# First half of w_in loaded in four pieces, V of the sixth pair behind a gate, three filler matmuls ahead of the first FFN product

## The chip, the cores and the metric

One core of one Trainium2 chip runs the whole program. The metric is the device time of one launch in microseconds (us). Before the change it is 332.88 us, the median of three runs (332.18 to 333.69).

## What is computed

A windowed attention with eight global tokens feeds a feed-forward layer (FFN) with a squared ReLU. Inputs and output are float32; the kernel works in bf16 on TensorE.

```python
# q, k, v: (8, 8, 576, 64); global_idx: 8 of the 576 positions
scores = q @ k.T / 8
mask = |i - j| <= 32  or  i is global  or  j is global
attn = softmax(where(mask, scores, -1e9)) @ v
x = attn.transpose(0, 2, 1, 3).reshape(4608, 512)
h = x @ w_in                              # w_in: (512, 2048)
out = (s * relu(h) ** 2 + b) @ w_out      # w_out: (2048, 512)
```

## The kernel before, in words

The 64 heads are 32 pairs (`NPAIR`), eight batches of four pairs. For each pair K and Q are brought into transposed form, `qk` (L666) makes the scores, ACT takes their exponential and DVE multiplies them by the mask (L673, L674), and `pvq` (L690) multiplies by V, two pairs at a time, in two column blocks, first with a block of ones (`onesb`) for the row sums, then with `vring`, the V of five pairs in bf16. The result is scaled into `xt` (L737), x transposed, 128 rows of the model dimension by tokens, in four row blocks `a`. The eight global tokens are put into `xt` by `scatter` on POOL (L762), eight copies per call.

The FFN runs beside the attention: `moe_quanta` (L770 to L860) is a generator of small portions. For each of nine blocks of 512 tokens there are sixteen products `psh` with `w_in` (L785, four matmuls each, over the row blocks `a`), a ReLU on ACT, a square on DVE, and then the products `pso` with `w_out` (L826). In the first block the products f = 0 to 3 are begun early: four portions ("leads") take the row blocks a = 0, 1, as soon as the first two pairs are in `xt`, and the row blocks 2, 3 follow later.

The order of each engine's work is that of the code (manual schedule). The opening (L1037 to L1165) is written out by hand: pairs 0 to 3, then `put_out(1, 1)`, two leads, `select(4)`, `trans_a(5)`, a lead, `qk(4, 0)`, a lead, `trans_b(5)`, `select(5)`, `qk(4, 1)`, a lead. From pair 4 on a table of steps rules (`run_pair`; eight steps per pair, one FFN portion in most). In that table `VLOAD`, `VROUND` and `VGLOBAL` say in which (pair, step) V of a pair is loaded on SP's queue, rounded to bf16 on POOL, and given its global rows.

DMA: POOL's queue (software, q0) brings the weights and the early K and Q with a cast to bf16; SP's queue (hardware, q1) brings V and the later K and Q. Both hold at most eight transfers in flight: each issue waits for the landing of the one eight before it. `win_t[0]` holds the columns 0 to 1023 of w_in (f = 0 to 7), `win_t[1]` the others; each is loaded in two pieces, row blocks 0, 1 (g = 0) and row blocks 2, 3 (g = 1). A `gate` is a DMA of one element on SP's queue that reads what an engine writes, so that what stands behind it in the queue starts only after that. V of pairs 4 and 5 is staged in two slots of `natk`; ACT rounds V of pair 5 at step (5, 2) (`cast_v`, L332). `warm(n)` (L989 to L993) issues n matmuls of zeros of 512 columns into an idle bank.

The names that matter below: `psv`, `psx`, `po` (L554, L690) are the last attention products ahead of the leads; `gf`, `gb`, `psg` (L415, L531, L539) are the gathered global rows of K and Q of the second group of pairs, their rounding on DVE and their transposes on TensorE, at step (7, 7); `gvall` is the V of the global rows.

Of the kernel before, what the change touches and what calls it, by code (L numbers as in the profile page):

```python
# [48 lines left out]
    8: (7, 0), 9: (7, 3), 10: (9, 0), 11: (9, 3), 12: (10, 4), 13: (11, 0), 14: (12, 3), 15: (12, 7),  # L49
# [3 lines left out]
    (12, 1): (1, 13), (13, 4): (1, 14), (14, 0): (1, 15),  # L53
}
VGLOBAL = {
    8: (8, 6), 9: (9, 0), 10: (10, 5), 11: (10, 7), 12: (12, 0), 13: (12, 3), 14: (13, 7), 15: (14, 2),
# [48 lines left out]
def kernel(  # L105
# [100 lines left out]
    win_t = [wpool.tile([P, 4, DF // 2], BF16, name=f"win{i}", tag=f"win{i}") for i in range(2)]  # L206
    wout_t = wpool.tile([P, 16, DM], BF16)
# [148 lines left out]
    gate = const.tile([1, 2], BF16)  # L356
# [8 lines left out]
    for p in range(6):  # L365
        load_v(nc.sync, p)
        if p == 3:
            nc.sync.dma_start(
                out=natk[0:NG, 2:4].rearrange("p n c h d -> p (n c h d)"),
                in_=bass.AP(  # L370
                    tensor=v.tensor, offset=v.offset,
                    ap=[[2 * NCH * 2 * D, NG], [1, 2 * NCH * 2 * D]],
                ),
            )
# [395 lines left out]
    def moe_quanta():  # L770
        for t in range(NTOK // 512):
# [10 lines left out]
            def into(psh, f, heads):  # L782
                for a in heads:
                    for j, (x0, d0, n) in enumerate(cols):
                        nc.tensor.matmul(  # L785
                            psh[:, d0 : d0 + n],
                            win_t[f // 8][:, a, 2 * P * (f % 8 // 2) :][:, 0 : 2 * P]
                            .rearrange("p (x t) -> p t x", t=2)[:, f % 2],
                            xt[:, a, x0 : x0 + n],
                            start=(a == 0 and j == 0), stop=(a == 3),  # L790
                            skip_group_check=True,
                        )
# [235 lines left out]
    def load_w_in(j, parts):  # L1028
        x = slice(1024 * j, 1024 * j + 1024)
        for g in parts:  # L1030
            nc.gpsimd.dma_start(out=win_t[j][:, 2 * g : 2 * g + 2], in_=w_in2[:, g, :, x])

# [12 lines left out]
    load_w_in(0, (0,))  # L1045
    load_kq(5)
    load_w_in(0, (1,))
# [51 lines left out]
    load_w_in(1, (0,))  # L1099
    muls[2]()  # L1100
    mask_b()
    gv_out()
    scatter(0, 0)
    warm(2)
# [15 lines left out]
    load_w_in(1, (1,))  # L1120
# [4 lines left out]
    open_batch(1)  # L1125
    lead()
# [19 lines left out]
    nc.sync.dma_start(out=gate[:, 1:2], in_=xgs[0][0:1, 2, 0:1])  # L1146
# [175 lines left out]
```

## Time and profile before

| | before |
|---|---|
| median of three runs | 332.88 us (332.18 to 333.69) |
| the profiled execution, its own time | 333.04 us |
| its span, first to last instruction | 331.1 us |
| TensorE (PE) busy | 317.5 us, 96% of the span |
| VectorE (DVE) busy | 210.0 us, 63% |
| ScalarE (ACT) busy | 197.3 us, 60% |
| GpSimd (POOL) busy | 121.4 us, 37% |
| moved by DMA | 49.48 MB, mean 149 GB/s |
| mean granted TensorE clock | 0.983 of full speed |

The profile is of one execution, 0.16 us above the median; its span leaves 1.94 us of its time outside. A busy share is an average over stages with different limits: TensorE is busy nearly throughout, but a matmul at half the clock is busy for twice as long, so the granted clock has to be read beside the busy time. "Idle before" names how long an engine stood still before an instruction and what ended that.

### The profile page before, as it was taken

How to read it: one execution, taken by the hardware profiler on the slowest of the kernel's cores; microseconds unless marked ns; L12 is line 12 of the kernel's file. 1: busy time of each engine (PE TensorE's matmuls, PEld its weight loads, DVE VectorE, ACT ScalarE, POOL GpSimd, SP SyncE). 2: the span in 40 equal slices, each digit the busy share in tenths (PEclk: the TensorE clock that was granted, in tenths of full speed). 3: DMA queues.
4: the chain of work that ended last, by engine and by line, in shares of the span. 5: the costliest groups of instructions: out<-in, count | busy, mean ns of one | idle time of the engine just before them, and what ended most of it. 6: DMA issues, size and time to landing. Idle time of an engine off the chain costs nothing.

```text
span 331.1 us, 8894 instructions
## 1 busy us (share of the span) xinstructions
PE 317.5 (96%) x3429; PEld 169.9 (51%) x3466; DVE 210.0 (63%) x539; ACT 197.3 (60%) x332; POOL 121.4 (37%) x237
## 2 busy tenths in 40 slices
PE   7977999999999999999999999999999999999996
PEld 5753445445454544478544444444466544444444
DVE  6893777687865885587568666776676624323422
ACT  3873885559865786678656875786378306404700
POOL 7397424221513542356344235845560220000000
PEclk9995799999999999999999999999999999999999
DMA  8999999999999999999999959997970210011012
GB/s 150 182 191 208 209 201 195 198 184 173 191 175 191 215 192 191 221 177 177 182 211 159 130 103 238 226 192 148 131 181 2 95 66 32 2 64 63 2 45 82
DMA packets 125674, 49.48 MB, mean 149 GB/s; under 512 B 114168, under 2 KB 119736, under 8 KB 125624
## 3 DMA queue, kind: packets, MB, share of 16 engines
q1 hardware_dynamic: 94030, 27.49, 50.8%
q0 software_dynamic: 31248, 21.00, 35.6%
q8 instruction: 27, 0.44, 0.6%
q10 hardware_dynamic: 354, 0.43, 0.5%
q14 instruction: 15, 0.12, 0.1%
HBM read 42.22 MB, written 9.44 MB: 156 GB/s over the span
## 4 chain that ended last, share of the span: by engine, by line
PE 84%; DMA 8%; SPq 2%; issue 2%; DVE 1%; ACT 1%; POOL 1%; POOLq 0%
PE psh L785 38%; PE pso L826 34%; PE po L690 5%; PE pss L666 3%; DMA win<-in_moe_w_in_dram 3%; DMA vring<-gvall 2%; DMA natv<-in_v_dram 2%; DMA sixk<-in_k_dram 1%; SPq L246 1%; PE psw L666 1%; PE pst L616 1%; PE pst L610 1%; ACT em L673 0%; PE pst L973 0%; POOL vring L332 0%
## 5 line engine op out<-in xcount | busy, mean ns | idle before, releaser
L785 PE MATMUL psh<-xt,win 128*128 128x512 bf16 (+4 forms) x687 | 132.3, 344 | 3.3 <-DMA win<-in_moe_w_in_dram 1.8
L826 PE MATMUL pso<-wout_t,g 128*128 128x512 bf16 (+1 forms) x573 | 126.5, 373 | 2.4 <-issue 2.1
L808 ACT ACTIVATE r<-psh 128x512 bf16<-128x512 f32 x144 | 85.9, 600 | 57.2 <-PE psh L785 45.0
L785 PEld LDWEIGHTS <-win 128*128 128x128 bf16 x704 | 63.8, 99 | 60.3 <-issue 3.3
L826 PEld LDWEIGHTS <-g 128*128 128x128 bf16 x592 | 56.1, 98 | 62.8
L811 DVE TENSOR_TENSOR g<-r 128x512 bf16<-128x512 bf16 x144 | 60.9, 428 | 33.6 <-ACT r L808 32.9
L674 DVE TENSOR_TENSOR em<-em,mask 128x904 bf16<-128x904 bf16 (+1 forms) x64 | 40.2, 632 | 35.8 <-ACT em L673 30.8
L673 ACT ACTIVATE em<-pss 128x840 bf16<-128x840 f32 (+1 forms) x37 | 32.7, 883 | 44.6 <-PE pss L666 44.6
L848 DVE SCALAR_TENSOR_TENSOR osb<-pso,sb,wst 128x512 f32<-128x512 f32 (+1 forms) x21 | 15.2, 724 | 28.0 <-PE pso L826 27.8
L246 POOL DMA_DIRECT2D vring<-in_v_dram x33 | 29.5, 897 | 8.6 <-PE po L690 7.0
L737 DVE TENSOR_TENSOR xt<-po,rep 128x480 bf16<-128x480 f32 (+2 forms) x60 | 24.5, 449 | 3.3 <-ACT rep L747 3.3
L762 POOL COPY xt<-xg 128x4 bf16 (+1 forms) x72 | 17.4, 242 | 15.9 <-DVE xt L737 12.0
L673 ACT ACTIVATE em<-psw 128x904 bf16<-128x904 f32 x23 | 21.2, 924 | 0.0
L1165 POOL DMA_DIRECT2D wst<-in_moe_w_out_dram x16 | 9.1, 575 | 31.7 <-DVE wsum L1171 23.5
L666 PEld LDWEIGHTS <-kt 64*128 64x128 bf16 x384 | 12.2, 100 | 15.4 <-issue 12.3
L332 POOL CAST vring<-natv 128x640 bf16<-128x640 f32 x12 | 8.7, 723 | 31.0 <-DMA natv<-in_v_dram 19.8
L690 PE MATMUL po<-em,vring 128*32 128x160 bf16 (+3 forms) x840 | 18.1, 221 | 0.9 <-POOL vring L566 0.5
L1183 POOL DMA_DIRECT2D out_dram<-osbh x13 | 7.4, 570 | 31.6 <-DVE osbh L1182 30.9
L257 ACT CAST natb<-natk 128x640 bf16<-128x640 f32 x22 | 15.9, 724 | 0.9 <-DMA natk<-in_k_dram 0.9
L744 ACT ACTIVATE ln<-po 128x324 f32<-128x324 f32 (+1 forms) x30 | 12.9, 430 | 4.5 <-PE po L690 4.5
L666 PE MATMUL pss<-qt,kt 64*128 64x192 bf16 (+4 forms) x222 | 14.4, 243 | 1.0 <-DVE grow L402 0.4
L747 ACT ACTIVATE rep<-ln 128x324 f32<-128x324 f32 (+1 forms) x32 | 14.8, 462 | 0.4
(128 smaller groups left out, 267.6 us busy)
## 6 DMA issues: line engine op xcount, KB each, us to landing
natk<-in_k_dram SPq DMA_DIRECT2D x45, 150.0 KB, 21.8
natv<-in_v_dram SPq DMA_DIRECT2D x28, 150.0 KB, 4.9
natq<-in_q_dram SPq DMA_DIRECT2D x55, 75.0 KB, 4.8
wst<-in_moe_w_out_dram POOLq DMA_DIRECT2D x16, 256.0 KB, 4.2
out_dram<-osbh POOLq DMA_DIRECT2D x13, 256.0 KB, 3.3
out_dram<-osb POOLq DMA_DIRECT2D x12, 256.0 KB, 3.0
natq<-in_q_dram SPq DMA_DIRECT2D x9, 288.0 KB, 6.5
vring<-in_v_dram POOLq DMA_DIRECT2D x31, 75.0 KB, 4.6
```

Of the source, the lines that this page charges most:

```text
L246: eng.dma_start(out=dst[r : r + rows, n, c : c + nch, hh], in_=bass.AP(tensor=src[t].tensor, offset=o + c * KC * D, ap=[[D, rows], [KC * D ...
L257: (nc.gpsimd.tensor_copy if p == NSIX else nc.scalar.copy)(out=natb[:, p % NV].rearrange("p (c h d) -> p c h d", c=NCH, h=2), in_=natk[:, ...
L666: nc.tensor.matmul(ps[:, hh, at : at + hi - lo], ktile[p][r, P * c : P * c + P], qbufs[p % 3][r, lo:hi], start=at == 0, stop=at + hi - lo ...
L673: nc.scalar.activation(em[:], ps[:, :, 0:n], AF.Exp, scale=SCALE)
L674: later.append(lambda: nc.vector.tensor_mul(em[:], em[:], masks[g]))
L690: nc.tensor.matmul(po[DH * j : DH * j + DH, a : a + n], view(vring[:, p % NVR, c, hh, part - 1 :], [2, DH]) if part else onesb[:], emt[(p, ...
L737: nc.vector.tensor_tensor(out=view(xt[:, 2 * g, x0 + t0 :], [NXT, 2], [w, runs], [1, w]), in0=view(po[:, STEP[blk] + col :], [STEP[blk], 2 ...
L762: nc.gpsimd.tensor_copy(out=xt[:, h, S * (bi % NX) : S * (bi % NX) + S][:, :, ds(greg_p[i], 1)], in_=xgs[bi][:, h, i : i + 1],)
L785: nc.tensor.matmul(psh[:, d0 : d0 + n], win_t[f // 8][:, a, 2 * P * (f % 8 // 2) :][:, 0 : 2 * P] .rearrange("p (x t) -> p t x", t=2)[:, f ...
L808: nc.scalar.activation(r[:], psh, AF.Relu)
L811: later.append(lambda g=g, r=r: nc.vector.tensor_mul(g[:], r[:], r[:]))
L826: nc.tensor.matmul(pso[:, 0:nn], gl[f][:, u * P : u * P + P], wout_t[:, f, n0 : n0 + nn], start=(f == 0), stop=(f == 15),)
```

## The change

The first half of w_in comes in four pieces instead of two: by row blocks (g) and by 512 columns (c). In `win_h` each piece is one contiguous stretch of `win_t[0]`; f = 0 to 3 read c = 0, f = 4 to 7 read c = 1. The first two pieces stand where the two old ones stood on POOL, the third where the first piece of the second half stood, the fourth and that first piece behind `scatter(0, 0)`. V of pair 5 is taken out of the opening's loads and put behind a gate on the first half of the global results of batch 0 (`xgs[0]`). Three fillers stand on TensorE between `put_out(1, 1)` and the first lead. For pair 13 V is loaded, rounded and given its global rows one to two steps earlier.

```diff
 VLOAD = {
-    8: (7, 0), 9: (7, 3), 10: (9, 0), 11: (9, 3), 12: (10, 4), 13: (11, 0), 14: (12, 3), 15: (12, 7),
+    8: (7, 0), 9: (7, 3), 10: (9, 0), 11: (9, 3), 12: (10, 4), 13: (10, 7), 14: (12, 3), 15: (12, 7),
 }
 VROUND = {
...
-    (12, 1): (1, 13), (13, 4): (1, 14), (14, 0): (1, 15),
+    (12, 0): (1, 13), (13, 4): (1, 14), (14, 0): (1, 15),
 }
 VGLOBAL = {
-    8: (8, 6), 9: (9, 0), 10: (10, 5), 11: (10, 7), 12: (12, 0), 13: (12, 3), 14: (13, 7), 15: (14, 2),
+    8: (8, 6), 9: (9, 0), 10: (10, 5), 11: (10, 7), 12: (12, 0), 13: (12, 2), 14: (13, 7), 15: (14, 2),
 }
...
+    win_h = win_t[0][:].rearrange("p a f -> p (a f)").rearrange("p (c a f) -> p c a f", c=2, a=4)
...
-    for p in range(6):
+    for p in range(5):
         load_v(nc.sync, p)
...
-                            win_t[f // 8][:, a, 2 * P * (f % 8 // 2) :][:, 0 : 2 * P]
+                            (
+                                win_t[1][:, a, 2 * P * (f % 8 // 2) :]
+                                if f > 7
+                                else win_h[:, f // 4, a, 2 * P * (f % 4 // 2) :]
+                            )[:, 0 : 2 * P]
...
-    def load_w_in(j, parts):
-        x = slice(1024 * j, 1024 * j + 1024)
-        for g in parts:
+    def load_w_in(j, g, c=None):
+        if c is None:
+            x = slice(1024 * j, 1024 * j + 1024)
             nc.gpsimd.dma_start(out=win_t[j][:, 2 * g : 2 * g + 2], in_=w_in2[:, g, :, x])
+            return
+        x = slice(DM * c, DM * c + DM)
+        nc.gpsimd.dma_start(out=win_h[:, c, 2 * g : 2 * g + 2], in_=w_in2[:, g, :, x])
...
     cast_v(G, 2)
-    load_w_in(0, (0,))
+    load_w_in(0, 0, 0)
     load_kq(5)
-    load_w_in(0, (1,))
+    load_w_in(0, 1, 0)
...
     put_v(G, 3)
-    load_w_in(1, (0,))
+    load_w_in(0, 0, 1)
     muls[2]()
     mask_b()
     gv_out()
+    nc.sync.dma_start(out=gate[:, 1:2], in_=xgs[0][0:1, 0, 0:1])
+    load_v(nc.sync, 5)
     scatter(0, 0)
+    load_w_in(0, 1, 1)
+    load_w_in(1, 0)
     warm(2)
     put_out(1, 0)
...
     load_kq(6, "q")
-    load_w_in(1, (1,))
+    load_w_in(1, 1)
...
     open_batch(1)
+    fill[0] = bank("psf")
+    warm(3)
     lead()
     lead()
```

**TensorE, between the last products of pair 3 (`psx`) and the first lead (`psh`).** The words in brackets name what a row waits for: a DMA of POOL's queue (DMASW), POOL, ACT. Before:

```order
L690 LDWEIGHTS vring
L690 MATMUL psx<-em_625,vring 32x136
L785 LDWEIGHTS win_122 [waits DMASW1_49]
L785 MATMUL psh<-xt,win_122 128x512 [waits Pool_49]
L785 LDWEIGHTS win_122
```

Now:

```order
L691 MATMUL psx<-em_623,vring 32x136
L998 LDWEIGHTS dummy
L998 MATMUL psf<-dummy 128x512
L998 LDWEIGHTS dummy
L998 MATMUL psf<-dummy 128x512
L998 LDWEIGHTS dummy
L998 MATMUL psf<-dummy 128x512
L786 LDWEIGHTS win_122 [waits Activation_49,DMASW1_49]
L786 MATMUL psh<-xt,win_122 128x512 [waits Pool_49]
```

Three fillers that wait for nothing stand ahead of the lead, which still waits for one piece of w_in and for POOL's eight copies into `xt`.

**POOL, at the end of the first `scatter` (`xt<-xg`; ISA rows set its column).** Before:

```order
L762 COPY xt<-xg_736 128x2 [waits Pool_49]
L219 DMA sixk<-in_k_dram 96x2x384 [waits DMASW6_49,PE_49]
L762 ISA
L762 COPY xt<-xg_736 128x2 [waits DVE_49]
L762 ISA
```

Now:

```order
L763 COPY xt<-xg_734 128x2 [waits Pool_49]
L1039 DMA win_122<-in_moe_w_in_dram 128x2x512 [waits DMASW6_49]
L1036 DMA win_123<-in_moe_w_in_dram 128x2x1024 [waits DMASW7_49]
L220 DMA sixk<-in_k_dram 96x2x384 [waits DMASW0_49,PE_49]
L763 ISA
L763 COPY xt<-xg_734 128x2 [waits DVE_49]
```

Two issues of w_in stand between the first and the second `scatter` that were ahead of the first before (one of them as a whole piece).

**SP's queue, at the end of the opening's loads of V (`natk` holds V of pairs 4 and 5).** Before:

```order
L246 DMA natk<-in_v_dram 120x5x64 [waits DMAHW2_49]
L246 DMA natk<-in_v_dram 120x5x64 [waits DMAHW3_49]
L375 DMA natk<-in_v_dram 8x1280 [waits DMAHW4_49]
L1146 DMA gate<-xg 1x1 [waits DMAHW5_49,DVE_49]
L246 DMA natv<-in_v_dram 120x5x64 [waits DMAHW6_49,Pool_49]
```

Now:

```order
L376 DMA natk<-in_v_dram 8x1280 [waits DMAHW2_49]
L1111 DMA gate<-xg 1x1 [waits DMAHW3_49,DVE_49]
L247 DMA natk<-in_v_dram 120x5x64 [waits DMAHW4_49]
L247 DMA natk<-in_v_dram 120x5x64 [waits DMAHW5_49]
L1160 DMA gate<-xg 1x1 [waits DMAHW6_49,DVE_49]
L247 DMA natv<-in_v_dram 120x5x64 [waits DMAHW7_49,Pool_49]
```

The two transfers of V of pair 5 have moved behind a gate of their own, and the old gate follows them.

## Rows read from the trace of the kernel before

**Rows 1.** The page's granted TensorE clock, tenths of full speed, 40 slices of 8.3 us.
```profile
PEclk9995799999999999999999999999999999999999
```

**Rows 2.** Stretches: us, busy per engine (x instructions), PEclk, DMA share, GB/s.
```profile
14.00:18.00 4.00, 3.60 (x82) 2.88 (x86) 3.00 (x7) 2.93 (x5) 3.14 (x5) 1.00 1.01 217
20.00:22.00 2.00, 1.15 (x34) 0.63 (x24) 1.92 (x8) 1.82 (x5) 1.94 (x4) 1.00 0.99 180
24.00:26.00 2.00, 0.73 (x38) 0.52 (x37) 1.44 (x7) 1.93 (x5) 1.34 (x7) 1.00 1.17 196
26.00:28.00 2.00, 1.04 (x3) 0.43 (x4) 1.07 (x4) 0.00 (x0) 1.29 (x5) 0.58 1.20 212
28.00:36.00 8.00, 7.78 (x94) 3.83 (x94) 3.09 (x11) 3.44 (x5) 6.26 (x13) 0.50 1.18 214
```

**Rows 3.** TensorE's timeline, 24 to 38 us: start, us, instruction [idle before, releaser].
```profile
24.35 0.57 PE L690 MATMUL psx<-em,vring 128*32 128x92 bf16 x28
26.74 0.61 PE L785 MATMUL psh<-xt,win 128*128 128x512 bf16 x1 [1.83 <-DMA win<-in_moe_w_in_dram]
...
37.05 0.37 PE L666 MATMUL pss<-qt,kt 64*128 64x160 bf16 x6
```

**Rows 4.** The chain that ended last, at full clock: start, us, what.
```profile
37.42 1.83 PE psh L785 x8
39.25 0.29 PE pss L666 x6
39.54 0.38 PE pst L616 x12
...
41.99 0.38 PE pst L973 x24
```

**Rows 5.** POOL's timeline, 18 to 30 us.
```profile
18.20 0.73 POOL L1031 DMA_DIRECT2D win<-in_moe_w_in_dram  x1
...
22.35 0.72 POOL L1031 DMA_DIRECT2D win<-in_moe_w_in_dram  x1
23.20 2.51 POOL L762 COPY xt<-xg 128x2 bf16 x8
...
27.16 1.97 POOL L762 COPY xt<-xg 128x2 bf16 x8 [0.47 <-DVE xt L737]
```

**Rows 6.** DMA issues at 18.2 and at 22.35 us: KB, us to landing.
```profile
win<-in_moe_w_in_dram POOLq DMA_DIRECT2D x1, 512.0 KB, 8.5
...
win<-in_moe_w_in_dram POOLq DMA_DIRECT2D x1, 512.0 KB, 11.5
```

**Rows 7.** Around the second group's global rows: POOL, DMA issues of 50 to 55 us, DVE, TensorE.
```profile
50.83 0.56 POOL L1227 DMA_DIRECT2D gvall<-in_v_dram  x1 [1.94 <-DMA wout_t<-in_moe_w_out_dram]
...
55.87 1.64 POOL L1227 DMA_DIRECT2D gvall<-in_v_dram  x3 [2.44 <-DMA wout_t<-in_moe_w_out_dram]
...
gvall<-in_v_dram POOLq DMA_DIRECT2D x3, 6.0 KB, 5.9
...
59.74 0.22 DVE L531 CAST gb<-gf 128x128 bf16<-128x128 f32 x1
...
60.02 0.25 PE L539 MATMUL psg<-ident,gb 64*64 64x64 bf16 x4
```

**Rows 8.** V, K, gate: DVE's and ACT's timeline, two DMA issue groups, one TensorE wait.
```profile
22.02 0.40 DVE L730 TENSOR_TENSOR xg<-tot,rec 128x16 bf16<-128x16 f32 x1
...
38.49 0.74 ACT L332 CAST vring<-natk 128x640 bf16<-128x640 f32 x1
...
60.23 0.72 ACT L257 CAST natb<-natk 128x640 bf16<-128x640 f32 x1 [0.86 <-DMA natk<-in_k_dram]
...
68.95 0.87 ACT L673 ACTIVATE em<-pss 128x840 bf16<-128x840 f32 x1 [4.22 <-PE pss L666]
...
natk<-in_v_dram SPq DMA_DIRECT2D x4, 150.0 KB, 5.9
...
natk<-in_k_dram SPq DMA_DIRECT2D x45, 150.0 KB, 21.8
...
PE po L690 <- DMA vring<-gvall: 0.4, 1, 0.4
```

More of the change, by code (lines that the diff above doesn't have):

```diff
@@ L355 @@
     load_kq(1)
-    gate = const.tile([1, 2], BF16)
+    gate = const.tile([1, 3], BF16)
     nc.sync.dma_start(out=gate[:, 0:1], in_=six["k"][0:1, 1, 0, 0, 0:1])
@@ L1145 @@
     lead()
-    nc.sync.dma_start(out=gate[:, 1:2], in_=xgs[0][0:1, 2, 0:1])
+    nc.sync.dma_start(out=gate[:, 2:3], in_=xgs[0][0:1, 2, 0:1])
     load_v(nc.sync, 6)
```

## The prediction

> **What bounds the kernel now.** I read the slices of the page first. TensorE is busy from end to end except in the first 33 us, and there the row of the granted clock falls: 0.5 in the fourth slice and 0.7 in the fifth, that is somewhere between 25 and 41 us, and full speed in every slice after [rows 1]. So the program is bound by TensorE, and the one place where TensorE works badly is the opening. The stretches sharpen it: 1.00 up to 26 us, 0.58 between 26 and 28, 0.50 from 28 to 36 [rows 2]. That is the step from 2.4 to 1.2 GHz. Ahead of the fall TensorE did little: 1.15 us of 2 between 20 and 22, and 0.73 us of 2 between 24 and 26, the emptiest stretch; from 28 on it was busy 7.78 of 8 us, all at half speed [rows 2].
>
> The timeline tells why it was empty. The last `psx` products end at 24.92; the first lead starts at 26.74, after 1.83 us of waiting for the first piece of w_in [rows 3]. That piece was issued at 18.20 and took 8.5 us [rows 5, 6]: 26.7. So one late DMA costs 1.8 us itself, and the half clock behind it costs more. From the first lead to the first score product of pair 5, whose start is 37.05, TensorE needs 10.3 us [rows 3].
>
> **The same work at full clock.** Sixteen `psh` matmuls, two `select`, two sets of transposes, two `qk`. Eight `psh` take 1.83 us, a `qk` 0.29, a set of transposes 0.38, a `select` 0.38 [rows 4]. Sum: 2 x 1.83 + 2 x 0.29 + 2 x 0.38 + 2 x 0.38 = 5.8 us, against 10.3.
>
> **The change, step by step.**
>
> *First piece of half the size.* 256 KB instead of 512 behind the same queue. It cannot land earlier than half of 8.5 us after 18.20, at 22.5, nor later than the whole one, at 26.7. I take 24.5, the middle, because V of pair 5 no longer competes then. The lead has a second condition: the eight copies of `scatter(0, 0)`, which run from 23.20 to 25.71 [rows 5]. The issue of the third piece in front of them replaces one of the same 0.72 us, so they stay. The lead starts at 25.75: **1.0 us** earlier. Only a landing after 25.7 would take from this.
>
> *Three fillers.* No operand to wait for, so they start at 24.92. Eight matmuls of this width take 1.83 us [rows 4], three take 0.7: 24.92 to 25.6, in a hole that exists anyway. They cost nothing, and what covers them is the wait for the copies; if copies and piece came earlier, the price is at most 0.7 us. What they buy: the stretch from 24 to 26 then has 0.73 + 0.7 + 0.25 = 1.7 us of work in 2, more than the 1.15 us of 20 to 22, at which the clock stayed at 1.00 [rows 2]. I take it that the clock holds. This is the main term.
>
> *The trace against a rule on transposes.* Between 14 and 18 us, with transposes and narrow products and hardly anything wide, the clock stayed at 1.00 [rows 2]; the work behind the leads is of the same mix with wide matmuls added, so I expect it to hold there too. The row of 28 to 36 us, nearly full and still at 0.50, leaves a doubt. The Trainium skill ("TensorE: Matmul & The Clock Gate", Part 4: PE-mode transpose) states that transposes do not count as TensorE activity in the way matmuls do; by that rule the clock could fall behind the fillers as well, among the transposes of pair 5, and the sum would keep 1.0 us only. That is in the third case below.
>
> *Two more issues on POOL, and two moved.* The fourth piece and the first piece of the second half now stand behind the first `scatter`: 2 x 0.72 us ahead of K of pair 6 and of the second `scatter`. It started at 27.16 after 0.47 us of idling, and took 1.97 [rows 5]; POOL was free for it at 26.7. Now it is free at 26.7 + 1.45 = 28.15, and done at 30.1 to 30.2. TensorE wants it for the lead on row blocks 2, 3: 25.75 + half the psh (1.83) + the other 2.1 = 29.7. So a new wait of **0.5 us**, ending on POOL. The eight matmuls left (1.83) end at 32.0, against 37.1 before: **5.0 us** earlier.
>
> *The later pieces.* Queue order in bytes is as before up to the first piece of the second half, which landed at 22.35 + 11.5 = 33.85 [rows 5, 6]. The fourth quarter lies 512 KB ahead of that. From 26.7 to 33.85 the queue moved K and Q of pair 5 (144 KB each) and two pieces of w_in, 1.3 MB in 7.15 us, so 512 KB take 2.8 us: the fourth quarter lands at 31.0, against 32.3 when f = 4 wants it. Even at 33.85 the wait would be 1.5 us, and what follows takes more than that back anyway. I charge nothing.
>
> *V of pair 5.* Its two transfers of 150 KB leave the stretch before 23 us and return behind the gate, when the first global results of batch 0 are written, at 22.4 [rows 8]. No bytes are saved; they move out of the way of the first piece. Transfers of V took 5.9 us to land, the longest of SP's K loads 21.8 [rows 8]; nearest is V itself. Landing is then about 30, and ACT rounds it at 38.49 before [rows 8], at 33.5 now: hidden. The old gate waits for a result that comes no earlier than before, so the loads behind it keep their place.
>
> *Pair 13.* TensorE waited 0.4 us for its global rows [rows 8]. They are issued a step earlier and ahead of 300 KB of V of pair 14, so I take the whole **0.4 us** back (bounds 0 and 0.4).
>
> **What is late next.** Five microseconds ahead, TensorE meets the DMA queues, which work near their limit: 212 to 214 GB/s here [rows 2], and the change saves no byte. POOL's queue goes on delivering in the same order at the same rate. The place where this binds first is the gathered K and Q of the second group of pairs (`gf`). They stand on the queue between the last piece of w_out, whose landing released POOL at 55.87, and the `gvall` row issued at 50.83, which landed after 5.9 us, at 56.7 [rows 7]. So `gf` lands between 55.6 and 56.7; I take 56.3. Before, nobody felt it: DVE rounded at 59.74, the transposes `psg` ran at 60.02 [rows 7]. Now TensorE would come to `psg` at 55.0; with the landing at 56.3 and 0.3 us from rounding to transposes it gets there at 56.6. Of the 5.0 us, **3.4** remain (3.0 to 4.1 over the bounds), whatever small waits occur before.
>
> Behind it ACT waits longer for K of pair 10: it came 0.86 us late for a cast at 60.23 [rows 8] and will be 4.3 us late. ACT has an idle stretch of 4.2 us ahead of 68.95 [rows 8], so most of that is covered. For this and for loads up to 125 us I charge **0.5 us** (0 to 2).
>
> **Sum.** 3.4 + 0.4 - 0.5 = 3.3 us less than the profiled execution's 333.04: **329.7 us**. (Its 333.04 is 0.16 above the median.)
>
> **The rivals.**
>
> *Loads keep up.* If the queues deliver earlier because TensorE asks earlier, `gf` does not bind and 5.0 + 0.4 us stay: 327.6. For: SP's queue waits for engines at many places, above all later. Against: POOL's queue does not wait for TensorE in the opening, so its landings have no reason to move. Chance 0.12.
>
> *The clock falls all the same*, at the same place or among the transposes of pair 5. Then some 10 us at half speed stay and only the earlier start counts: 333.04 - 1.0 = 332.0. For: 28 to 36 us [rows 2], and three narrowly sized fillers. Against: the 20 to 22 us row. Chance 0.18.
>
> *The supply takes it back*: the clock holds, but K, Q and V of pairs 8 to 15 are as late as before, and ACT's 4.3 us are covered by half only. 333.04 - 3.8 + 2.2 = 331.4. For: the cast at 60.23 already waits. Against: it is the only such wait of ACT on a load in the table period that I find, and TensorE's own sum of waits for DMA there is 0.4 us. Chance 0.07.
>
> *V of pair 5 comes late: slower.* Its issue moves behind 22.4, and with the gate and two issues of some 0.7 us each the second transfer is out at 23.9; from then it shares with POOL's queue. If it needs what the slow K loads needed, 21.8 us [rows 8], it lands at 45.7; ACT, which works in order, stands at the cast from 38.5 on, the exponentials and ReLUs behind it, and TensorE with them: 7 us lost against before, about 340. It decides from a landing of 38.5 on, that is 14.6 us from issue. For: the slow loads went through the same queue. Against: V in the same opening took 5.9 [rows 8], and behind it in the queue nothing older is left. Chance 0.05.
>
> **How the numbers follow.** Likeliest, with chance 0.58: 329.7, its own range 328.5 to 331.5, from the bounds of `gf` (3.0 to 4.1), all or nothing of the 0.4, and up to 1.5 of the 2 us for later loads. The range for 8 in 10 takes in the fallen clock (332.0 with 0.2 for its spread) and reaches to 327.7, half into the case in which all is kept: 327.7 to 332.2. A measurement of this kernel tells about 0.5% from no change, 1.7 us: 331.2 and 334.5 are the marks. Faster: 0.58 + 0.12 and a little of the third rival, 0.72. Slower: 0.05 and a remainder, 0.06. The same: 0.22, nearly all of it the fallen clock.
>
> **What would show it.** Right: granted clock 1.00 in every slice after 24 us; fillers at 24.9; first lead at 25.7 to 25.8, released by POOL's copies and not by w_in; pair 5's first score product near 32; a wait of TensorE or DVE that ends on `gf` at 56 to 57; no wait for `vring` of pair 13. Wrong on the main term: a stretch at 0.50 after 26 us. Wrong on the clamp: `psg` well before 56. Wrong on V: an ACT cast of `natk` near 34 that waits for a DMA.

## The result, and the profile after

The changed kernel takes 333.90 us (median of 22 runs, 332.46 to 335.72), the kernel before, run beside it, 331.65 (22 runs, 329.19 to 334.52). The ratio is 1.0062, with a 95% interval of 1.0041 to 1.0083: **slower by 0.6%**, where 329.7 us were forecast and 332.2 was the end of the range. The profiled execution of the changed kernel took 334.58 us, its span is 332.9. The medians here and below are of all runs, while the ratios leave out four single runs that lie over 1.5% above the fastest of their kernel (two of six in e16, one of twelve in e13 and in e20).

The opening went as foretold. The page's row of the granted clock has no dip any more (before: [rows 1]):

```profile
PEclk9999999999999999999999999999999999999999
```

The stretches of the changed kernel (us, busy time of each engine, PEclk, DMA share, GB/s), against [rows 2]:

```profile
22.00:24.00 2.00, 1.78 (x66) 1.24 (x67) 1.97 (x6) 0.92 (x3) 1.81 (x4) 1.00 1.06 123
24.00:26.00 2.00, 1.46 (x43) 0.93 (x42) 1.48 (x6) 1.97 (x5) 1.52 (x8) 1.00 1.23 187
26.00:28.00 2.00, 2.00 (x42) 1.10 (x40) 1.66 (x10) 0.23 (x2) 2.00 (x3) 1.00 1.21 215
28.00:36.00 8.00, 6.30 (x78) 3.08 (x78) 5.34 (x13) 7.17 (x13) 6.39 (x16) 1.00 1.18 202
```

From 24 to 36 us every stretch has 1.00, the higher of the two levels, where the profiled execution of the kernel before had 0.50. But the last column is new: from 22 to 24 us the DMA engines are as busy as ever (share 1.06) and move 123 GB/s. In the kernel before, the same two microseconds had 1.08 and 198 GB/s:

```profile
22.00:24.00 2.00, 1.44 (x52) 1.06 (x53) 1.98 (x5) 0.85 (x3) 1.82 (x4) 1.00 1.08 198
```

TensorE's timeline of the changed kernel (start, us, instruction, idle before and releaser), against [rows 3] and the `psg` row of [rows 7]:

```profile
25.19 0.59 PE L998 MATMUL psf<-dummy 128*128 128x512 bf16 x2 [0.16 <-issue]
25.88 1.02 PE L786 MATMUL psh<-xt,win 128*128 128x512 bf16 x4
...
30.39 1.67 PE L786 MATMUL psh<-xt,win 128*128 128x512 bf16 x7 [0.17 <-POOL xt L763]
32.20 0.37 PE L667 MATMUL pss<-qt,kt 64*128 64x160 bf16 x6
...
36.33 0.45 PE L617 MATMUL pst<-ident,sixk 96*64 96x96 bf16 x12 [1.40 <-DMA sixk<-in_k_dram]
...
58.00 0.25 PE L540 MATMUL psg<-ident,gb 64*64 64x64 bf16 x4 [0.88 <-DVE gb L532]
```

The first lead starts at 25.88 and not at 26.74, pair 5's first score product at 32.20 and not at 37.05: 4.85 us ahead. At `psg` 2.0 of them are left (58.00 against 60.02), although DVE's cast ahead of it now waits for `gf` itself:

```profile
57.67 0.27 DVE L532 CAST gb<-gf 128x128 bf16<-128x128 f32 x1 [0.70 <-DMA gf<-in_q_dram,grow]
```

Behind it the lead turns into a lag. The first `psw` product of pairs 11, 12 and 14 in the kernel before, by TensorE's timeline:

```profile
91.07 0.37 PE L666 MATMUL psw<-qt,kt 64*128 64x160 bf16 x6
...
97.84 0.36 PE L666 MATMUL psw<-qt,kt 64*128 64x160 bf16 x6
...
114.81 0.36 PE L666 MATMUL psw<-qt,kt 64*128 64x160 bf16 x6
```

and in the changed kernel:

```profile
91.97 0.37 PE L667 MATMUL psw<-qt,kt 64*128 64x160 bf16 x6
...
100.22 0.36 PE L667 MATMUL psw<-qt,kt 64*128 64x160 bf16 x6
...
116.58 0.37 PE L667 MATMUL psw<-qt,kt 64*128 64x160 bf16 x6
```

0.90 us behind at pair 11, 2.38 at pair 12, 1.77 at pair 14, and 1.78 at the last such product (249.63 against 247.85). So 6.6 us are lost between 32 and 115 us, and nothing after it. TensorE's four longest waits from 28 to 110 us name where 5.1 of them go (us in total, times, longest):

```profile
PE psw L667 <- DVE kt L578: 1.6, 2, 0.9
PE pst L617 <- DMA sixk<-in_k_dram: 1.4, 1, 1.4
PE po L691 <- DMA vring<-gvall: 1.2, 1, 1.2
PE psg L540 <- DVE gb L532: 0.9, 1, 0.9
```

In the kernel before, the only wait for a load there is the 0.4 us of [rows 8].

### The profile page after: what moved, and what is told of

The parts are those of the page before. It is cut to its first block, busy times and chain, and to the rows that moved or that the text cites. A ratio compares the mean times of both kernels' runs of the same rounds, so it can differ in the third digit from the quotient of the medians.

```text
span 332.9 us, 8905 instructions
## 1 busy us (share of the span) xinstructions
PE 315.7 (95%) x3431; PEld 169.4 (51%) x3469; DVE 209.7 (63%) x539; ACT 197.8 (59%) x332; POOL 124.1 (37%) x239
## 4 chain that ended last, share of the span: by engine, by line
PE 74%; DMA 10%; SPq 6%; issue 3%; POOL 3%; DVE 1%; ACT 1%; POOLq 0%; DVEq 0%; ACTq 0%
PE pso L831 33%; PE psh L786 32%; PE po L691 5%; DMA sixk<-in_k_dram 4%; SPq L247 4%; DMA natk<-in_k_dram 3%; DMA natv<-in_v_dram 2%; PE pss L667 2%; DMA vring<-gvall 2%; SPq L287 1%; PE psw L667 1%; POOL win L1039 1%; ACT r L813 1%; POOL xt L763 1%; PE pst L611 1%
## 5 line engine op out<-in xcount | busy, mean ns | idle before, releaser
L786 PE MATMUL psh<-xt,win 128*128 128x512 bf16 (+4 forms) x687 | 129.3, 340 | 1.3 <-issue 0.3
L675 DVE TENSOR_TENSOR em<-em,mask 128x904 bf16<-128x904 bf16 (+1 forms) x64 | 39.4, 621 | 35.4 <-ACT em L674 33.0
L691 PEld LDWEIGHTS <-vring 128*32 128x32 bf16 x896 | 14.1, 99 | 2.3 <-issue 1.4
```

The costliest lines, as they stand in the source:

```text
L675: later.append(lambda: nc.vector.tensor_mul(em[:], em[:], masks[g]))
L691: nc.tensor.matmul(po[DH * j : DH * j + DH, a : a + n], view(vring[:, p % NVR, c, hh, part - 1 :], [2, DH]) if part else onesb[:], emt[(p, ...
L786: nc.tensor.matmul(psh[:, d0 : d0 + n], (win_t[1][:, a, 2 * P * (f % 8 // 2) :] if f > 7 else win_h[:, f // 4, a, 2 * P * (f % 4 // 2) :]) ...
```

## The experiments

Times are medians, and each ratio is to runs of the kernel before on the same chip. A landmark that all profiles have is the first `psw` product of a pair.

### Which part of the change costs

**e1**, the changed kernel with V of pair 5 back in the opening:

```diff
-    for p in range(5):
+    for p in range(6):
...
-    nc.sync.dma_start(out=gate[:, 1:2], in_=xgs[0][0:1, 0, 0:1])
-    load_v(nc.sync, 5)
```

> The changed kernel with V of pair 5 back among the opening's loads and without its gate; all else as changed. Theory S (supply: the DMA engines bind from about 30 to 107 us, and the gate left them short of work between 20 and 24 us, 162 and 123 GB/s against 180 and 198 before, some 0.24 MB or 1.2 us): 1.0 to 1.6 us faster than the changed kernel, and the transposes of K of pair 9, issued at 62.4 in the changed kernel, are issued near 61. Theory T (the table edits for pair 13 are what costs): within 0.4 us of the changed kernel.

Measured: 334.61 us, ratio 1.0092 (1.0055 to 1.0129). Nothing is regained. The hole in the rate, that is the stretch with few GB/s, is still there at another place: 116 GB/s from 28 to 30 us in place of 123 from 22 to 24. V of pair 5 behind its gate is not the loss.

**e2**, the changed kernel with the three entries of pair 13 as before:

```diff
-    ... 12: (10, 4), 13: (10, 7), ...
+    ... 12: (10, 4), 13: (11, 0), ...
...
-    (12, 0): (1, 13), ...
+    (12, 1): (1, 13), ...
...
-    ... 13: (12, 2), ...
+    ... 13: (12, 3), ...
```

> The changed kernel with the three table entries for pair 13 as they were before. Theory T (V of pair 13 now stands on SP's queue ahead of the global rows of pair 11, for which TensorE waited 1.25 us at 92.7): that wait goes, and the time falls by 0.8 to 1.3 us. Theory S: TensorE is held by the DMA supply as a whole, the wait comes back at a later load of the same stretch, and less than 0.5 us is won.

Measured: 333.06, ratio 1.0041 (1.0016 to 1.0065), 0.8 below the changed kernel. TensorE's wait for `gvall` rows is 0.2 us instead of 1.2. The two ratios alone do not tell the kernels apart, since their intervals overlap. The runs of e1 to e4, all on one chip, do: the fifteen with the entries (e1, e4) have a mean 1.1 us above the twenty-four without (e2, e3), with a 95% interval of 0.4 to 1.7, though the four differ in V of pair 5 and in the fillers as well. The entries cost; they were credited with a gain.

**e3**, the four pieces and the fillers alone (the edits of e1 and e2 together):

> Only the four pieces of w_in and the three fillers, V of pair 5 and the table as before. Theories S and T together: 2.0 to 2.8 us faster than the changed kernel, so at or a little under the kernel before. If the held clock were worth its full 4.5 us after all and nothing else bound: 4 us under the kernel before.

Measured: 333.29, ratio 1.0042 (1.0017 to 1.0068). So most of the loss against the kernel before is in the pieces.

**e4**, the changed kernel without `fill[0] = bank("psf")` and `warm(3)`:

> The changed kernel without its three fillers. Theory C (the held clock is worth what the stretch at half clock cost, some 4.5 us): the clock falls again after 26 us and the time rises by 3 to 5 us. Theory S: even if the clock falls, TensorE only arrives later at waits for DMA that it has anyway, and the time stays within 0.7 us of the changed kernel.

Measured: 334.29, ratio 1.0066 (1.0038 to 1.0093), level with the changed kernel. Its first lead starts no earlier or later than in the changed kernel, and without fillers the row shows what it waited for:

```profile
25.89 1.02 PE L786 MATMUL psh<-xt,win 128*128 128x512 bf16 x4 [0.84 <-POOL xt L763]
```

In five of its eight runs the mean granted clock was 0.998 or more, in two 0.990 or less; these two took 333.34 and 334.84 us, no more than the others. So in these two runs a fallen clock cost nothing that shows. Two of eight is also not far from the third of the runs in which the clock of the kernel before falls (46 of 136, below): eight runs do not tell whether the earlier lead helps the clock.

### The edits on the kernel before

**e5**, the kernel before with six fillers ahead of the first lead and nothing else:

```diff
     open_batch(1)
+    fill[0] = bank("psf")
+    warm(6)
     lead()
```

> The kernel before with nothing but six fillers ahead of the first lead (six, since its wait there is longer). It holds the clock in every run. Theory C (the held clock is worth its 4.5 us): 3 us or more under the median before. Theory S (the DMA engines bind to about 107 us, and the runs of before that keep their clock by themselves are only about 1.2 us faster than those in which it falls): 0.2 to 0.6 us under the median before, and TensorE waits at K of pair 9 and V of pairs 8 and 9 as it does in the changed kernel.

Measured: 331.16, ratio 0.9977 (0.9956 to 0.9999): a version that beats the kernel before by little (the interval ends just short of 1) and the changed one clearly. Its lead starts at 26.62, no earlier than before, and its first score product of pair 5 comes at 32.57. Its waits from 28 to 110 us:

```profile
PE psg L539 <- DVE gb L531: 1.5, 1, 1.5
PE pss L666 <- ACT em L673: 0.4, 1, 0.4
PE po L690 <- DVE xt L737: 0.2, 1, 0.2
```

2.1 us, against 5.1 in the four rows of the changed kernel. The held clock alone gives this much, and the rest of the change takes it away.

**e6**, the kernel before with the first piece of the second half moved behind the scatter:

```diff
-    load_w_in(1, (0,))
     muls[2]()
...
     scatter(0, 0)
+    load_w_in(1, (0,))
```

> The kernel before with one line moved: the first piece of the second half of w_in is issued behind the first scatter instead of ahead of it; pieces whole, no fillers, V of pair 5 and the table as before. Theory D (dry queue: with 0.5 to 0.77 MB of w_in issued only behind the scatter, POOL's DMA queue runs out of work between 23 and 30 us, and the DMA engines never get that time back): DMA moves 0.1 to 0.3 MB less between 20 and 36 us than before, and the time rises by 0.7 to 1.5 us. Theory P (the smaller pieces with rows half as long cost DMA time): no change, within 0.4 us.

Measured: 331.87, ratio 0.9995 (0.9969 to 1.0021), and 3.35 MB moved from 20 to 36 us: the expected loss did not come. One whole piece may stand behind the scatter.

**e7**, e3 with the fourth piece and the first of the second half issued ahead of the scatter:

```diff
     load_w_in(0, 0, 1)
+    load_w_in(0, 1, 1)
+    load_w_in(1, 0)
...
     scatter(0, 0)
-    load_w_in(0, 1, 1)
-    load_w_in(1, 0)
```

> The kernel of e3_win_fill (four pieces, fillers) with the fourth piece and the first piece of the second half issued ahead of the first scatter instead of behind it. The scatter and with it the first lead start some 1.4 us later, near 27.3. Theory D: the queue no longer runs dry, 3.2 to 3.3 MB between 20 and 36 us, and the time falls by 0.8 to 1.6 us against e3_win_fill in spite of the later lead. Theory P: as slow as e3_win_fill, or slower by the later lead.

Measured: 332.29, ratio 1.0014 (0.9989 to 1.0039), 1.0 below e3, and 3.13 MB from 20 to 36 us. The intervals overlap, so that the place of the two issues is about half of the loss is likely, and not shown by this run alone. A hole is left: 128 GB/s at a share of 1.06 from 22 to 24 us.

**e8**, four pieces, but each two where the whole one stood, V and pair 13 as before:

```diff
     load_w_in(0, 0, 0)
+    load_w_in(0, 0, 1)
     load_kq(5)
     load_w_in(0, 1, 0)
+    load_w_in(0, 1, 1)
...
-    load_w_in(0, 0, 1)
+    load_w_in(1, 0)
...
     scatter(0, 0)
-    load_w_in(0, 1, 1)
-    load_w_in(1, 0)
```

> As e7_issues_ahead, but each pair of quarter pieces stands where the whole piece stood before (both column halves of row blocks 0, 1, then of row blocks 2, 3), the second half in its old place. Theory D: as the kernel before, within 0.5 us. Theory P: 1.0 us or more slower than the kernel before, as e3_win_fill is.

Measured: 331.32, ratio 1.0003 (0.9975 to 1.0030); its runs spread from 329.90 to 334.27, so the ratio says more than the median. I read it as "small pieces cost nothing", and that was too quick: its profile has 3.18 MB from 20 to 36 us against 3.36 in e5, and its interval leaves room for 0.9 us.

### Bytes, runs and order

A run is a stretch of consecutive addresses within a transfer. The sizes of runs, pieces and packets are those of the bf16 numbers that land; in DRAM, where w_in is float32, the same run is twice as long.

Up to here I thought that POOL's queue ran dry while POOL did the scatter. The rows speak against it. All packets of the changed kernel from 22 to 24 us, and those of POOL's queue (packets, MB, share of the 16 engines):

```profile
DMA packets 286, 0.25 MB, mean 123 GB/s; under 512 B 20, under 2 KB 285, under 8 KB 285
...
q0 software_dynamic: 285, 0.23, 103.2%
```

and of the kernel before from 28 to 30 us, where POOL's queue is alone as well:

```profile
DMA packets 222, 0.42 MB, mean 212 GB/s; under 512 B 15, under 2 KB 15, under 8 KB 222
...
q0 software_dynamic: 222, 0.42, 112.9%
```

By their share the engines are full both times. 285 packets at 103% of 16 engines in 2 us are 116 ns each, for 0.8 KB; 222 at 113% are 163 ns each, for 1.9 KB: in the first stretch a byte costs 1.7 times as much. Short runs by themselves do not do that. The next two microseconds of the changed kernel, 24 to 26 us, have nothing but short packets of POOL's queue either:

```profile
DMA packets 446, 0.37 MB, mean 187 GB/s; under 512 B 31, under 2 KB 446, under 8 KB 446
...
q0 software_dynamic: 446, 0.37, 122.6%
```

These are 88 ns each for 0.8 KB, 1.2 times the price of a byte in the long runs. So a hole takes short runs and something else beside them; the runs below show that the time of the issues matters, and no run shows by what mechanism.

**e13**, the changed kernel with the pieces read in runs of 2 KB:

```diff
-        x = slice(DM * c, DM * c + DM)
-        nc.gpsimd.dma_start(out=win_h[:, c, 2 * g : 2 * g + 2], in_=w_in2[:, g, :, x])
+        nc.gpsimd.dma_start(
+            out=win_h[:, c, 2 * g : 2 * g + 2].rearrange("p a f -> p (a f)"),
+            in_=w_in2[:, g, c, 0 : 2 * DM],
+        )
```

> The changed kernel with its four pieces in their places and of their sizes, but each read from DRAM as runs of 2 KB (1024 columns of one row) in place of two runs of 1 KB (512 columns of two rows). The weights that land are then not the ones of the reference: it is a kernel for the time alone. Theory R (the short runs cost: in the changed kernel's 22 to 24 us 285 packets, nearly all under 2 KB, held the 16 engines for 103% of the time and carried 0.25 MB, in the kernel before 222 packets of about 2 KB carried 0.42 MB at 113% from 28 to 30 us; that is 116 ns for a short packet and 163 ns for a long one, so 1024 short ones in place of 512 long ones take 7.4 us of the 16 engines in place of 5.2): the hole at 22 to 24 us fills, 20 to 36 us carry some 3.2 to 3.3 MB in place of 2.99, and the time falls by 1.0 to 2.2 us, to 331.7 to 332.9. Theory D (POOL's queue has too little ahead of the first scatter, the issue times decide): nothing changes, 333.9 and 2.99 MB.

Measured: 333.26, ratio 1.0047 (1.0021 to 1.0073), 3.11 MB: half of what theory R (short runs cost) expected in bytes, and 0.6 us where it expected 1.0 or more. By its interval the time need not have changed.

**e14**, e5 with whole pieces of the first half, read in runs of 1 KB:

```diff
+            if not j:
+                nc.gpsimd.dma_start(
+                    out=win_t[0][:, 2 * g : 2 * g + 2].rearrange("p a (c f) -> p (a c) f", c=2),
+                    in_=w_in2[:, g].rearrange("p h (c f) -> p (h c) f", c=2)[:, :, 0:DM],
+                )
+                continue
```

> The kernel before with the six fillers ahead of the first lead (331.2 us), its first half of w_in still in two pieces of 512 KB where they stood, but each read as runs of 1 KB (512 columns of each 1024) in place of 2 KB. The second 512 columns are not the reference's: it is a kernel for the time alone. Theory R: the bytes of 20 to 36 us fall from 3.36 to about 3.0 MB, and the time rises by 1.0 to 2.2 us, to 332.2 to 333.4. Theory D: the same issues at the same times, so 331.2 and 3.36 MB.

Measured: 330.74, ratio 0.9970 (0.9949 to 0.9992), 3.32 MB. Short runs by themselves cost nothing that can be told where the other pieces stand early and whole. R alone falls.

**e9**, e5 with 0.52 MB more on POOL's queue in pair 6:

```diff
+        if p == 6:
+            wpieces(0)
```

> The kernel before with the six fillers (331.2 us) and two loads more of 256 KB each on POOL's queue at the start of pair 6, into buffers that are loaded again later and which nothing reads in between; the output is the reference's. If the DMA engines set the pace from 35 to 107 us, 0.52 MB at 204 GB/s take 2.6 us of it, of which TensorE's own work may still hide some: 331.7 to 333.8. If the transfers have room there and only single waits count, 331.2 within 0.4.

Measured: 333.50, ratio 1.0054 (1.0029 to 1.0078): 2.3 us more than e5 by the medians (2.3 and 2.8 more than e11 and e14, which ran on the same chip as e9), where the bytes at 204 GB/s, the rate of the kernel before from 28 to 60 us, are 2.6. Its longest waits from 28 to 110 us are for a transposed K and for w_in:

```profile
PE psw L666 <- DVE kt L577: 1.8, 1, 1.8
PE psh L785 <- DMA win<-in_moe_w_in_dram: 0.8, 1, 0.8
```

The clock fell for a while in that profile (0.83 from 66 to 76 us), but the six runs with a mean clock of 0.998 or more have a median of 333.01, so the price is not the clock's. That gives the frame: with TensorE at full clock, transfers set the pace here, and bytes put on POOL's queue at pair 6 cost nearly their whole time.

**e11**, e5 with the gather of `gf` ahead of the last piece of w_out:

```diff
     load_kq(8)
+    gather(1)
     load_w_out(3)
...
-                if i == 2:
-                    gather(1)
```

> The kernel before with the six fillers (331.2 us), and the global rows of the next batch (the gather into gf) issued ahead of the last load of w_out in place of behind two global rows of V. In the kernel with the fillers TensorE's one long wait from 28 to 110 us is 1.5 us at psg for those rows. If that wait is a loss of its own: psg without it, and 329.7 to 330.5. If the DMA engines are what binds, the 1.5 us come back at later loads: 331.2 within 0.4.

Measured: 331.17, ratio 0.9980 (0.9955 to 1.0006), e5's time. The wait at `psg` is gone, and waits for `kt` (0.8 us), w_in (0.7) and `gvall` (0.5) stand in its place: which load comes late can be chosen, not that one does.

**e15**, e7 with e13's runs of 2 KB, that is both halves of the loss mended in one kernel:

> The kernel of four pieces and fillers with the fourth piece and the first of the second half issued ahead of the first scatter, as it ran at 332.29 us and 3.13 MB from 20 to 36 us, its four pieces now read in runs of 2 KB (the weights that land are not the reference's: for the time alone). If late issues (0.17 MB) and short runs (0.12 MB) are two losses that add up: 3.25 to 3.35 MB, and 331.2 to 331.8, level with the kernel before with fillers (331.2). If one of them hides the other: 3.13 MB and 332.3, as without the long runs.

Measured: 331.57, ratio 0.9985 (0.9958 to 1.0013), 3.41 MB. Against e3 that is 1.9 us, and here the intervals do not overlap: late issues and short runs together account for the loss of the pieces. The bytes are above the 3.25 to 3.35 MB expected: the two mended halves give more than their sum (0.45 MB over e3, where 0.17 and 0.12 add to 0.29), as they would if a hole takes both. The same rows from 20 to 36 us, first the changed kernel:

```profile
DMA packets 4783, 2.99 MB, mean 187 GB/s; under 512 B 2594, under 2 KB 4489, under 8 KB 4780
...
q0 software_dynamic: 2333, 2.30, 94.6%
```

e13, long runs only:

```profile
DMA packets 4243, 3.11 MB, mean 194 GB/s; under 512 B 2556, under 2 KB 3339, under 8 KB 4240
...
q0 software_dynamic: 1826, 2.43, 93.4%
```

e7, early issues only:

```profile
DMA packets 4919, 3.13 MB, mean 196 GB/s; under 512 B 2694, under 2 KB 4550, under 8 KB 4916
...
q0 software_dynamic: 2371, 2.42, 96.0%
```

e15, both:

```profile
DMA packets 4740, 3.41 MB, mean 213 GB/s; under 512 B 2867, under 2 KB 3772, under 8 KB 4737
...
q0 software_dynamic: 2026, 2.66, 95.1%
```

and e5, whole pieces in their old places:

```profile
DMA packets 4792, 3.36 MB, mean 210 GB/s; under 512 B 2946, under 2 KB 3870, under 8 KB 4789
...
q0 software_dynamic: 1966, 2.58, 92.4%
```

POOL's queue holds the engines for 92 to 96% of these 16 us in all five. What differs is the price of a megabyte on it: 0.946 x 16 / 2.30 = 6.6 us in the changed kernel, 6.2 and 6.3 with one half mended, 5.7 with both and in e5.

Profiles of kernels with the same opening repeat these bytes: 2.98 to 3.00 MB in the changed kernel, e2, e10 and e18, and 3.28 to 3.36 in e5, e9, e11 and e20 (e16 and e19, where a cast on POOL was slow, have 3.41 and 2.67). The bytes also order the times of the kernels whose later loads are the same but for the order of a few (e11, pair 13). Taking e5 as the zero, 4.9 us for each megabyte fewer (204 GB/s) and 0.9 us where pair 13's entries are in (a value between e2's 0.7 by ratios and the 1.1 of e1 to e4):

| kernel | MB, 20 to 36 us | worked out, us over e5 | measured ratio less e5's, x 331.8 us |
|---|---|---|---|
| e15 | 3.41 | -0.2 | 0.3 |
| e6 | 3.35 | 0.0 | 0.6 |
| e14 | 3.32 | 0.2 | -0.2 |
| e11 | 3.32 | 0.2 | 0.1 |
| before | 3.28 | 0.4 | 0.8 |
| e8 | 3.18 | 0.9 | 0.9 |
| e7 | 3.13 | 1.1 | 1.2 |
| e2 | 3.00 | 1.8 | 2.1 |
| e3 | 2.96 | 2.0 | 2.2 |
| e10 (below; its V load is back, so without the 0.9) | 3.00 | 1.8 | 2.6 |
| e13 | 3.11 | 1.2 + 0.9 | 2.3 |
| after | 2.99 | 1.8 + 0.9 | 2.8 |
| e4 | 2.91 | 2.2 + 0.9 | 3.0 |
| e1 | 2.90 | 2.3 + 0.9 | 3.8 |

The bytes are of one profiled execution each, so a single line proves little (a ratio's interval is about 0.8 us to either side). Thirteen lines lie within 0.6 us and e10 within 0.8, so the order as a whole is hard to have by chance.

### Pair 13, and taking bytes away

**e10**, the changed kernel with only the V load of pair 13 back at `(11, 0)`:

> The changed kernel with pair 13's V loaded at pair 11's start, as before, its rounding and its global rows as the change has them. If V's issue ahead of the global rows of pair 11 on SP's queue is what makes TensorE wait 1.2 us for them: that wait back at 0.4 or less and 333.0 within 0.4, as with all three entries old (333.06). If it is the earlier rounding or the earlier rows of pair 13: 333.9 within 0.4.

Measured: 333.05, ratio 1.0055 (1.0024 to 1.0086). The median is the one expected if the load is the cause; the ratio lies nearer to the changed kernel's, and its interval does not tell 1.0041 from 1.0062. So the times leave open whether the load alone is the cause. The profile shows what the load does. In the changed kernel the chain of waits has

```profile
88.24 5.59 DMA vring<-gvall
```

behind two V loads on SP's queue:

```profile
87.13 0.99 SPq L247 DMA_DIRECT2D natv<-in_v_dram  x2
88.24 0.72 SPq L567 DMA_DIRECT2D vring<-gvall  x1
```

and in e10 the rows of pairs 10 and 11 are issued together, ahead of those loads:

```profile
86.17 1.63 SPq L567 DMA_DIRECT2D vring<-gvall  x2
...
91.30 1.53 SPq L247 DMA_DIRECT2D natv<-in_v_dram  x2
```

From pair 11's first `psw` to pair 12's it takes 6.76 us in e10 (91.88 to 98.64), as in the kernel before (6.77), and 8.25 in the changed kernel: 1.5 us.

**e16** and **e18**, e5 and the changed kernel with the `wst` loads moved out of the stretch:

```diff
-WPIECES = [ ((11, 1), ((12, 1), (12, 2))), ...
+WPIECES = [((14 + j, 1), ((14 + j, 6), (14 + j, 7))) for j in range(8)]
```

> The kernel before with the six fillers (331.2 us), and the eight pairs of wst loads, which are summed for the bias of the end, moved from pairs 11 to 20 to pairs 14 to 21, so that 1.05 MB less are moved ahead of 107 us; the sums are the reference's. If transfers set the pace there, TensorE gets back what it waits, which in the profile is 2.1 us from 28 to 110 us: 329.2 to 330.2. If only their bytes matter and not their place (they are then paid after 107 us): 331.2 within 0.4.

> The changed kernel (333.9 us) with the same wst loads moved to pairs 14 to 21. If its loss is that of supply from 35 to 107 us, the megabyte taken out there, 5.1 us at 204 GB/s, gives back its waits of 5.5 us but for those of pair 13's rows and of the psg transposition (0.9): 329.8 to 331.5, and psw of pair 14 at 113 us or before in place of 116.6. If the waits are of single loads that are late in their queue, whatever else is moved: 333.0 to 333.9.

Measured: 338.17 (ratio 1.0119, 1.0068 to 1.0169) and 339.86 (1.0246, 1.0200 to 1.0292). Both missed by far, and the profiles show a reason that was not in the expectation: five steps are too few for the load, and VectorE waits at the additions, 6.4 us in all in e16 and 7.2 in e18. e18 from 138 to 152 us:

```profile
DVE wsum L1176 <- DMA wst<-in_moe_w_out_dram: 2.9, 1, 2.9
```

In e18 pair 14's `psw` comes at 113.85 and not at 116.58, 2.7 us earlier. That is no sign that the missing megabyte gives time back. Pair 10's `psw` and the first of the moved loads in the changed kernel:

```profile
84.61 0.37 PE L667 MATMUL psw<-qt,kt 64*128 64x160 bf16 x6 [0.95 <-DVE kt L578]
...
87.90 1.23 POOL L1179 DMA_DIRECT2D wst<-in_moe_w_out_dram  x2
```

and pair 10's `psw` in e18:

```profile
82.49 0.37 PE L658 MATMUL psw<-qt,kt 64*128 64x160 bf16 x6
```

2.1 of the 2.7 us are there before the first load that was moved is issued.

**e19** and **e20**, the same with a step more for each load, and the first at pair 13:

```diff
+    ((13, 6), ((14, 4), (14, 5))),
+    ((14, 6), ((15, 4), (15, 5))),
...
+    ((20, 5), ((21, 3), (21, 4))),
```

> The changed kernel (333.9 us) with the eight pairs of wst loads at pairs 13 to 20, the last where it was, each six steps ahead of its first addition: 1.05 MB less ahead of 107 us, and in e18's manner, but with a step more for each load to land. If the loss is of supply: psw of pair 14 at some 114 us (116.58 in the changed kernel) as in e18, no wait for wst on the way, and 331.2 to 332.0. If what e18 lost later has nothing to do with the additions: 336 or more.

> The kernel before with the six fillers (331.2 us) and the same places for the wst loads. TensorE waits 2.1 us there from 28 to 110 us. If these are of supply: 329.2 to 330.5. If they are of single rows (1.5 us at psg for the gathered rows): 331.2 within 0.4.

Measured: 335.16 (1.0093, 1.0060 to 1.0125) and 331.44 (0.9982, 0.9953 to 1.0012). e20 is level with e5, which is the result expected of single rows and not of supply. It tests little, though: e5's one long wait for a load is at `psg`, at 57.68 us, and the first load that e20 moves is issued in e5 at 85.61. e19 decides nothing: in its profiled execution a cast of V on POOL took 2.70 us in the opening in place of 0.75, TensorE stood 2.6 us for it at 22 us, the clock fell, and pair 8 began 4.4 us late. From pair 8 to pair 14 it then took 45.5 us (49.1 in the changed kernel, 45.7 in e5), but 2.1 of these 3.6 us are gained up to pair 11, before the moved loads, and a late start relieves the loads too. So no run shows that taking bytes away gives time back; that bytes set the pace rests on e9 and on the table. Why POOL's cast was so slow there, and in e16's profile too, stays open.

## Why the prediction was wrong

**Right.** The clock at 1.00 through the leads and the transposes of pair 5; the lead at 25.88 (25.75 foretold), released by POOL's copies and not by w_in (e4's row at 25.89); the new wait on POOL at the other half of that lead (0.17 us at 30.39; 0.5 foretold); pair 5 at 32.20 ("near 32"); no price for V of pair 5, whose casts run without a wait at 31.51 and 34.37 (the 21.8 us that were read as the longest of SP's K loads [rows 8] are the median of 45, and nothing came to hang on them); `gf` as the load that meets TensorE at `psg`, though about a microsecond later (cast at 57.67) than the 56.7 that bounded it.

**The sum, term by term** (ratios to the kernel before, x 331.8 us): the fillers alone -0.8 (e5), the pieces +2.2 (e3 against e5), V of pair 5 and pair 13 together +0.7 (the changed kernel against e3), in all +2.1. The prediction had -3.4 for the earlier and faster opening, nothing for the pieces, -0.4 for pair 13 and +0.5 for later loads. It also started from 333.04, which it took to be 0.16 above the median; 22 runs put the median 1.39 below it.

**The step that failed: "The later pieces".** It took the byte order of POOL's queue as unchanged and so its landings as fixed, and "I charge nothing". It asked in which order the bytes stand, and not what a byte costs on its way. Pieces of 256 KB, in runs of 1 KB and issued at 18.30, 20.28, 22.47 and 25.95, in place of whole ones at 18.20 and 20.16, leave stretches with few GB/s: 2.99 MB from 20 to 36 us where the kernel before moved 3.28 and the one with fillers 3.36. POOL's timeline of the changed kernel, against [rows 5]:

```profile
22.47 0.72 POOL L1039 DMA_DIRECT2D win<-in_moe_w_in_dram  x1
23.31 2.52 POOL L763 COPY xt<-xg 128x2 bf16 x8
25.95 0.72 POOL L1039 DMA_DIRECT2D win<-in_moe_w_in_dram  x1
26.66 0.72 POOL L1036 DMA_DIRECT2D win<-in_moe_w_in_dram  x1
28.01 2.33 POOL L763 COPY xt<-xg 128x2 bf16 x8
```

Measured against e5, that is 0.37 MB, or 1.8 us at 204 GB/s; the times of e3 and e5 put it at 2.2 us. e15, with early issues and long runs, is back at e5's bytes and time. e7 and e13 mend a part each, by less than their intervals, so how the loss divides is not shown, nor what makes a packet dear in the holes.

**The clamp was one load; the bound was the queue.** I clamped the lead at `gf` and charged 0.5 us for every load after it. In e5 `gf` is indeed the one load that TensorE waits for between 28 and 110 us. But e11 shows that the wait is not its own: with `gf` early, other loads are waited for and the time stays. And e9 shows that 0.52 MB more are paid with 2.3 us. In the changed kernel, which is 0.37 MB behind e5, K, V and their global rows are waited for too. The text said it ("the DMA queues, which work near their limit") and gave the case in which the supply takes the lead back 0.07. That rival is the nearest to what came, which went further than it was worked out, since the prediction had not asked what the change does to the supply itself.

**Pair 13: 0.4 us of gain foretold, 0.7 to 1.1 of loss measured** (e2, and e1 to e4 on one chip). I counted whom the moved load is put ahead of among the later loads, and not among the earlier ones: it goes ahead of the global rows of pair 11 on SP's queue, and TensorE waits 1.2 us for these (e10's profile). Whether the load is all of it, the times do not tell.

**The clock's worth was read from one execution.** Its half clock from 28 to 36 us [rows 2] was taken as the kernel's habit. Of the 136 runs of the kernel before whose clock is on record, 46 have a mean granted clock of 0.990 or less (median 332.62 us), 61 one of 0.998 or more (331.20): the fall comes in about a third of the runs, and these are 1.4 us slower, where the prediction kept 3.4. A TensorE that keeps its clock meets a wait for a load instead (1.5 us at `psg` in e5's profile). So the largest term was worth 1.4 us in some runs, and e5 collects 0.8 on average. That the fillers hold the clock was right: a mean clock of 0.990 or less came in 51 of 156 runs without fillers ahead of the lead (before, e4, e6) and in 15 of 191 with them, nine of these in e16, e18 and e19, where VectorE and POOL hold TensorE up elsewhere.

**The rule on transposes.** The Trainium skill ("TensorE: Matmul & The Clock Gate", Part 4: PE-mode transpose) would have let the clock fall among them. The changed kernel's stretches from 26 to 36 us, with sets of transposes at 27.36 and 29.12 and four selections around them, stay at 1.00, so this trace does not show it.

## What to carry to other kernels

Before an engine is brought forward, ask by how much the loads behind it are ahead, as a sum of bytes over the stretch: if the queues run full, the gain ends at their lead, and bytes that the change itself delays can be paid nearly in full, as they were here (e9). A transfer cut in parts by columns has runs of half the length: look not only at whether the DMA engines are busy but at GB/s beside their share. And look at the clock of every run that is listed before one profile's dip is made the main term.

## What was not expected of the hardware

DMA engines with a full share and little throughput: POOL's queue alone with runs of 1 KB and less moved 123 GB/s at a share of 1.06 in the changed kernel (22 to 24 us), 116 at 1.07 in e1 and 140 at 1.23 in e3 (28 to 30 us), against 212 at 1.13 with packets of 2 KB. Yet the same short runs of POOL's queue moved 187 at 1.23 in the changed kernel from 24 to 26 us and 203 in e7 from 25 to 28, and beside SP's packets 197 in e14 from 22 to 24. So the length of the runs alone does not set the rate. The Trainium skill ("DMA: Bandwidth & Descriptors", Why small descriptors are slow) gives a fixed cost of some 3 cycles for each packet beside 8 for 256 bytes; an estimate from that is 3 in 35, 9%, at 1 KB. The rows of the holes have 1.7 times the time for a byte, so that rule does not account for them, and what does stays open.

The clock of one and the same program, the kernel before, fell to a mean of 0.990 or less in 46 of 136 runs, and in none of the twelve of e5.
